# Pooled attention in slots of one unit, inputs laid out features first, one reduction per pooling sum

## The chip, the core and the metric

One core of a Trainium2 chip. The metric is device time in microseconds, the median of the runs shown; less is better. Engines are named as the profile names them: PE is TensorE (PEld its weight loads), DVE VectorE, ACT ScalarE, POOL GpSimd, SP SyncE, which here issues every DMA.

## The reference

Attention over pooled keys and values, then two gated layers. All inputs and the output are float32; shapes and factors as used:

```python
B, H, S, D = 8, 8, 576, 64          # pool = 8, so 72 pooled positions
k_p = k.reshape(B, H, 72, 8, D).mean(axis=3)
v_p = v.reshape(B, H, 72, 8, D).mean(axis=3)
attn = softmax(q @ k_p^T / sqrt(D)); x = attn @ v_p      # -> x: 4608 x 512
h = x @ w_in;  x = (h * sigmoid(1.702 h)) @ w_out         # 512 -> 2048 -> 512
out = ((x @ w_a) * (x @ w_b)) @ w_o2                      # 512 -> 1536 -> 512
```

## The kernel before

The 4608 tokens are 9 blocks j of 512, and a block is 4 units u of 128 tokens. The hidden features are split over four passes (`passes`): pass 0 makes features 0 to 5 (in 128s) of the first layer for all 9 blocks, pass 1 features 6 to 15, passes 2 and 3 the second layer. One step of pass 0 is one block and one 128-feature f: 12 matmuls of 512 columns into `h` (`emit_h`, L112 to L114: each product is made of hi and lo parts, three matmuls), the gate on ACT and DVE (L374, L375, split into `ghi` and `glo` by L71 and L72), and 12 matmuls into the accumulators `acc` (`emit_y`, the same three lines).

Attention runs inside pass 0, one block ahead of the steps that use it; units 0 to 3 run before the first step. A unit has five stages. `stage_a`: PE transposes q (tile `qt`, L211), ACT copies it to `qT` (L213). `stage_b1`: scores `sc` on PE against block-diagonal pooled keys `kbd` (L227), maximum on DVE (L234, L235), eight exponentials with row sums on ACT (L238). `stage_b2`: DVE normalises the weights `at` (L247 to L249). `stage_c`: PE transposes them (tile `pt`, L258), ACT copies to `aT` (L259). `stage_d`: PE multiplies with the pooled values (tile `px`, L271), and ACT and DVE split the result into the block's `xhi` and `xlo` (L71, L72). A unit that spans two batches does its scores and values in two pieces.

Keys and values are pooled per batch. `kv_ops` loads the raw rows of two heads at a time into `kraw` (two buffers for keys and values together, L188), and `sum_positions` adds the eight positions by halving: 512, 256 and 128 elements (L172, L172, L174). `stage_k` transposes the summed keys on PE (tile `kt`, L203) and copies them into `kbd` (L204, L205).

The stages of all units stand in one list, `unit_ops`: per unit the groups b1; b2 and the next unit's a; c; d. `spread` deals the list of a block evenly over the six steps of the block before. Weights come as 64-bit words and are converted by `convert`: eight DVE operations and one on ACT per half of a 128-feature tile (L93 to L109). Six such tiles are needed by the end of block 0. Every engine works its queue in order; the order in a queue is fixed when the program is built. SP issues all loads and stores in one queue, too.

Of the kernel before, what the change touches and what calls it, by code (L numbers as in the profile page):

```python
# [24 lines left out]
def tile_kernel(ctx, tc, q, k, v, w_in, w_out, w_a, w_b, w_o2, out):  # L25
# [129 lines left out]
    def last_batch(u):
        return min(B - 1, ((u + 1) * P - 1) // S)

    def load_q(u):
        t = ap_.tile([P, H, D], F32, tag="q", name="q", bufs=2)
        for o, n, b, s in pieces(u):  # L160
            nc.sync.dma_start(out=t[o:o + n], in_=q[b, :, s:s + n, :].rearrange("h p d -> p h d"))
        q_t[u] = t

    def kv_tiles(b):
        ks_t[b] = ap_.tile([SP, H, D], F32, tag="ks", name="ks", bufs=1)
        vs_t[b] = ap_.tile([SP, H, D], F32, tag="vs", name="vs", bufs=2)

    def sum_positions(dst, raw):

        n = POOL // 2  # L170
        while n > 1:
            nc.vector.tensor_tensor(out=raw[:, :, 0:n, :], in0=raw[:, :, 0:n, :], in1=raw[:, :, n:2 * n, :], op=ALU.add)  # L172
            n //= 2
        nc.vector.tensor_tensor(out=dst, in0=raw[:, :, 0, :], in1=raw[:, :, 1, :], op=ALU.add)  # L174

    def positions(src, b, h, n):
        return src[b, h:h + n].rearrange("h (p r) d -> p h r d", r=POOL)

    def kv_ops(b):

        waiting = []

        def one(src, tiles, h):
            if src is k and h == 0:
                kv_tiles(b)
            if src is not None:
                raw = ap_.tile([SP, 2, POOL, D], F32, tag="kraw", name="kraw", bufs=2)
                nc.sync.dma_start(out=raw, in_=positions(src, b, h, 2))  # L188
                waiting.append((tiles, h, raw))
            if len(waiting) > 1 or src is None:  # L190
                tiles, h, raw = waiting.pop(0)
                sum_positions(tiles[b][:, h:h + 2, :], raw)

        todo = [(src, tiles, h) for src, tiles in ((k, ks_t), (v, vs_t)) for h in range(0, H, 2)]
        return [lambda a=a: one(*a) for a in todo + [(None, None, None)]]

    def stage_k(b):


        ks = ks_t.pop(b)  # L200
        pt = ps.tile([P, NP, SP], F32, tag="ps", name="kt")
        for c in range(NP):
            nc.tensor.transpose(pt[:, c, :], ks[:, 2 * c:2 * c + 2, :].rearrange("p h d -> p (h d)"), ident[:SP, :SP])  # L203
        nc.scalar.copy(out=kbd[b % 2][0:D, :, 0:SP], in_=pt[0:D])  # L204
        nc.scalar.copy(out=kbd[b % 2][D:P, :, SP:2 * SP], in_=pt[D:P])  # L205

    def stage_a(u):
        t = q_t.pop(u)
        pt = ps.tile([P, NP, P], F32, tag="ps", name="qt")
        for c in range(NP):  # L210
            nc.tensor.transpose(pt[:, c, :], t[:, 2 * c:2 * c + 2, :].rearrange("p h d -> p (h d)"), ident)  # L211
        s = ap_.tile([P, NP, P], F32, tag="qT", name="qT", bufs=2)
        nc.scalar.copy(out=s, in_=pt)  # L213
        qT_t[u] = s

    def stage_b1(u):
        qT = qT_t.pop(u)
        a = ap_.tile([P, H, SP], F32, tag="at", name="at", bufs=2)
        mx = ap_.tile([P, H], F32, tag="mx", name="mx", bufs=2)
        sm = ap_.tile([P, H], F32, tag="sm", name="sm", bufs=2)  # L220
        scale = 1.0 / (POOL * D ** 0.5)
        for half in range(2):
            sc = ps.tile([P, H // 2, SP], F32, tag="ps", name="sc")
            for c in range(2):
                pair = 2 * half + c
                for o, n, b, s in pieces(u):
                    nc.tensor.matmul(  # L227
                        out=sc[o:o + n, 2 * c:2 * c + 2, :].rearrange("p h k -> p (h k)"),
                        lhsT=qT[:, pair, o:o + n],
                        rhs=kbd[b % 2][:, pair, :],  # L230
                        start=True, stop=True,
                    )
            hs = slice(half * (H // 2), (half + 1) * (H // 2))
            nc.vector.tensor_reduce(out=mx[:, hs], in_=sc, op=ALU.max, axis=AX.X)  # L234
            nc.vector.tensor_scalar_mul(mx[:, hs], mx[:, hs], -scale)  # L235
            for c in range(H // 2):
                h = half * (H // 2) + c
                nc.scalar.activation(  # L238
                    out=a[:, h, :], in_=sc[:, c, :], func=AF.Exp, scale=scale, bias=mx[:, h:h + 1],
                    accum_out=sm[:, h:h + 1],  # L240
                )
# [20 lines left out]
    def stage_d(u):  # L262
# [5 lines left out]
        for c in range(NP):  # L268
            for e in range(2):
                for o, w, b, s in pieces(u):  # L270
# [12 lines left out]
    stages = {"a": stage_a, "b1": stage_b1, "b2": stage_b2, "c": stage_c, "d": stage_d}  # L283
    loaded_q, made_b = [0], [0]

    def loads_to(u):
        while loaded_q[0] <= min(u, NU - 1):
            load_q(loaded_q[0])
            loaded_q[0] += 1

    def keys_for(u):
        while made_b[0] <= last_batch(u):
            stage_k(made_b[0])
            made_b[0] += 1
# [3 lines left out]
    unit_ops = []  # L298
    for u in range(NU):
        unit_ops += [[("b1", u)], [("b2", u)] + ([("a", u + 1)] if u + 1 < NU else []), [("c", u)], [("d", u)]]  # L300
    for b in range(2, B):
        i = 4 * (b * S // P) - 14
        for n, op in enumerate(kv_ops(b)):
            unit_ops[i + n * 3 // 2].insert(0, op)

    def ops_of(j):

        return [op for i in range(4 * UB * j, 4 * UB * (j + 1)) for op in unit_ops[i]]

    def step(op):  # L310
        if callable(op):
            op()
            return
        kind, u = op
        stages[kind](u)
        if kind == "a":
            keys_for(u)
            loads_to(u + 2)
# [170 lines left out]
    for j in range(1, NB):  # L489
        spread(([("a", UB)] if j == 1 else []) + ops_of(j), place[0, j - 1, 0], place[0, j, 0] - 1)  # L490
# [49 lines left out]
    def load_raw(src, b, n):  # L540
        raws = []
        for h in range(0, H, n):
            raw = wp.tile([SP, n, POOL, D], F32, tag="w", name="kvraw")
            nc.sync.dma_start(out=raw, in_=positions(src, b, h, n))
            raws.append((h, n, raw))
        return raws

    tmps += [ap_.tile([P, 512], U32, tag="tmp", name="tmp", bufs=3) for _ in range(3)]
    kv_tiles(0)
    kraws = load_raw(k, 0, 2)  # L550
    loads_to(1)
# [3 lines left out]
    for h, n, raw in kraws:
        sum_positions(ks_t[0][:, h:h + n, :], raw)
    step(("a", 0))
    step(("a", 1))
    for h, n, raw in vraws:
        sum_positions(vs_t[0][:, h:h + n, :], raw)  # L560
    stage_b1(0)
    stage_b1(1)
    stage_b2(0)
    stage_c(0)
    step(("a", 2))
    stage_d(0)
    stage_b2(1)
    stage_c(1)
    stage_d(1)
    make_w((1, 0), 0)  # L570
    make_w((1, 0), 1)
    stage_b1(2)
    load_w((1, 2))
    step(("a", 3))
    stage_b2(2)
    stage_b1(3)
    stage_c(2)
    stage_d(2)
    stage_b2(3)
    stage_c(3)  # L580
# [63 lines left out]
```

## Time and profile before

| | |
|---|---|
| median of 3 runs | 1944.31 us (1940.04 to 1946.99) |
| the profiled execution | 1944.94 us, of which the span is 1943.1 us |
| PE busy | 1845.0 us (95%) |
| DVE busy | 871.9 us (45%) |
| ACT busy | 561.5 us (29%) |
| DMA | 206.97 MB in 111552 packets, 43608 of them under 512 B |

The span is cut into 40 slices of 48.6 us in the profile; a digit there is a busy share in tenths, and PEclk is the granted TensorE clock in tenths of 2.4 GHz. Idle time of PE matters only where PE then has less to do than time; so the text reads the clock, the idle time and what ended it by stretch. A PE record is longer than its pace, since matmuls overlap: the pace is the distance between starts, and the chain of waits shows it as the length of a piece. The trace has two records for a matmul on plain float32 (scores, values), one for the others.

### The profile page before, as it was taken

Reading aid. Unit: us, or ns where it says so; the run is one execution under the profiler, and the core shown is the slowest. Engines: PE = TensorE matmul, PEld = TensorE weight load, DVE = VectorE, ACT = ScalarE, POOL = GpSimd, SP = SyncE. Lnnn points to the kernel's source line nnn. Section 1 sums busy time; section 2 is a strip of 40 time slices with the busy share of each in tenths; the row PEclk is TensorE's granted clock in tenths of the full one; section 3 lists DMA queues with packets and bytes.
Section 4 is the critical chain, followed back from the end, with each engine's and each line's share of the span. In section 5 each row is a group of like instructions: output and inputs, shape, how many; then the busy total and the mean of one; then the engine's idle time right before and its main releaser. Section 6 shows DMA issues by size and latency. Waiting matters only on the chain.

```text
span 1943.1 us, 22159 instructions
## 1 busy us (share of the span) xinstructions
PE 1845.0 (95%) x8768; PEld 1509.1 (78%) x8768; DVE 871.9 (45%) x1654; ACT 561.5 (29%) x1381; POOL 1.7 (0%) x8
## 2 busy tenths in 40 slices
PE   3698899889999999999999999999999999999998
PEld 2576777667788888888888888888888888888887
DVE  8955666555556444444544354444622212221221
ACT  4354454445533222232222122222211111111111
POOL 0000000000000000000000000000000000000000
PEclk8799999899999999999999999999999999999999
DMA  8533343432271222333322353424022102210200
GB/s 222 172 122 85 123 144 129 140 108 84 94 272 65 99 97 98 119 130 119 130 98 98 120 184 106 165 97 163 22 87 87 60 27 87 87 54 33 87 22 22
DMA packets 111552, 206.97 MB, mean 107 GB/s; under 512 B 43608, under 2 KB 64088, under 8 KB 99928
## 3 DMA queue, kind: packets, MB, share of 16 engines
q1 hardware_dynamic: 111448, 205.55, 30.9%
q8 instruction: 69, 1.13, 0.3%
q14 instruction: 35, 0.29, 0.0%
HBM read 139.46 MB, written 66.06 MB: 106 GB/s over the span
## 4 chain that ended last, share of the span: by engine, by line
PE 86%; DVE 6%; DMA 5%; ACT 2%; SPq 1%; issue 0%; DVEq 0%; ACTq 0%
PE ab L112 10%; PE ab L113 10%; PE ab L114 10%; PE h L112 6%; PE acc L112 6%; PE acc L113 6%; PE h L113 6%; PE h L114 6%; PE acc L114 6%; PE acc L413 5%; PE acc L414 5%; PE acc L415 5%; DMA kraw<-in_k_dram 2%; DMA kraw<-in_v_dram 2%; PE px L271 1%; DVE kraw L172 1%
## 5 line engine op out<-in xcount | busy, mean ns | idle before, releaser
L112 PE MATMUL ab<-xhi,w 128*128 128x512 f32 x864 | 336.1, 389 | 0.0
L113 PE MATMUL ab<-xlo,w 128*128 128x512 f32 x864 | 336.1, 389 | 0.0
L114 PE MATMUL ab<-xhi,w 128*128 128x512 f32 x864 | 336.1, 389 | 0.0
L401 DVE TENSOR_TENSOR c<-c,ab 128x512 f32<-128x512 f32 x108 | 74.3, 688 | 529.6 <-PE ab L114 529.6
L112 PE MATMUL h<-xhi,w 128*128 128x512 f32 x576 | 229.1, 401 | 6.8 <-ACT xhi L71 6.6
L113 PE MATMUL acc<-glo,w 128*128 128x512 f32 x576 | 229.6, 399 | 2.3 <-DVE glo L72 2.1
L113 PE MATMUL h<-xlo,w 128*128 128x512 f32 x576 | 228.0, 396 | 2.7 <-DVE xlo L72 2.7
L114 PE MATMUL acc<-ghi,w 128*128 128x512 f32 x576 | 227.2, 394 | 0.0
L114 PE MATMUL h<-xhi,w 128*128 128x512 f32 x576 | 226.9, 394 | 0.0
L375 DVE SCALAR_TENSOR_TENSOR g<-g,h 128x512 f32<-128x512 f32 x144 | 98.6, 685 | 250.7 <-ACT g L374 250.1
L112 PE MATMUL acc<-ghi,w 128*128 128x512 f32 x576 | 179.7, 405 | 12.5 <-ACT ghi L71 11.8
L114 PEld LDWEIGHTS ab<-xhi,w 128*128 128x128 f32 x864 | 162.2, 188 | 33.7
L112 PEld LDWEIGHTS ab<-xhi,w 128*128 128x128 f32 x864 | 162.2, 188 | 33.7
L113 PEld LDWEIGHTS ab<-xlo,w 128*128 128x128 f32 x864 | 162.2, 188 | 33.5
L374 ACT ACTIVATE g<-h 128x512 f32<-128x512 f32 x144 | 86.3, 600 | 303.8 <-PE h L114 291.3
L413 PE MATMUL acc<-w,chi 128*128 128x512 f32 x432 | 168.0, 389 | 0.0
L414 PE MATMUL acc<-w,chi 128*128 128x512 f32 x432 | 168.0, 389 | 0.0
L415 PE MATMUL acc<-w,clo 128*128 128x512 f32 x432 | 167.6, 389 | 0.0
L400 ACT COPY c<-ab 128x512 f32<-128x512 f32 x108 | 63.6, 589 | 356.4 <-PE ab L114 356.4
L71 ACT CAST chi<-c 128x512 fp32r<-128x512 f32 x108 | 66.9, 620 | 288.8 <-DVE c L401 288.8
L112 PEld LDWEIGHTS acc<-ghi,w 128*128 128x128 f32 x576 | 107.7, 193 | 37.2 <-ACT ghi L71 16.8
L112 PEld LDWEIGHTS h<-xhi,w 128*128 128x128 f32 x576 | 109.3, 191 | 32.2 <-ACT xhi L71 8.6
(66 smaller groups left out, 2162.9 us busy)
## 6 DMA issues: line engine op xcount, KB each, us to landing
part<-ys SPq DMA_DIRECT2D x72, 256.0 KB
part<-part SPq DMA_DIRECT2D x18, 1024.0 KB
xhi<-yd SPq DMA_DIRECT2D x18, 1024.0 KB
xlo<-yd SPq DMA_DIRECT2D x18, 1024.0 KB
xd<-xhi SPq DMA_DIRECT2D x9, 1024.0 KB
xd<-xlo SPq DMA_DIRECT2D x9, 1024.0 KB
xhi<-xd SPq DMA_DIRECT2D x9, 1024.0 KB
xlo<-xd SPq DMA_DIRECT2D x9, 1024.0 KB
```

The costliest lines, as they stand in the source:

```text
L71: nc.scalar.copy(out=hi, in_=src)
L112: nc.tensor.matmul(out=o, lhsT=whi, rhs=xhi, start=first, stop=False)
L113: nc.tensor.matmul(out=o, lhsT=whi, rhs=xlo, start=False, stop=False)
L114: nc.tensor.matmul(out=o, lhsT=wlo, rhs=xhi, start=False, stop=last)
L172: nc.vector.tensor_tensor(out=raw[:, :, 0:n, :], in0=raw[:, :, 0:n, :], in1=raw[:, :, n:2 * n, :], op=ALU.add)
L374: nc.scalar.activation(out=g, in_=hps, func=AF.Tanh, scale=0.5 * 1.702)
L375: made = nc.vector.scalar_tensor_tensor(out=g, in0=g, scalar=1.0, in1=hps, op0=ALU.add, op1=ALU.mult)
L400: nc.scalar.copy(out=cc, in_=pab[0])
L401: made = nc.vector.tensor_tensor(out=cc, in0=cc, in1=pab[1], op=ALU.mult)
L413: nc.tensor.matmul(out=o, lhsT=chi[:, cs], rhs=whi, start=first, stop=False)
L414: nc.tensor.matmul(out=o, lhsT=chi[:, cs], rhs=wlo, start=False, stop=False)
L415: nc.tensor.matmul(out=o, lhsT=clo[:, cs], rhs=whi, start=False, stop=last)
```

## The change

Before the launch the arrays are laid out anew on the host (`_laid_out`): q and k with features on the partitions, v with the eight positions innermost, and w_in, w_a, w_b so that a 128-feature tile is 4 KB in a row per partition. The bytes stay the same. In the kernel:

- `stage_a`, `stage_k`'s transposes and `qT` are gone: q is loaded as the scores need it, and `kbd` is filled from the sums.
- A pooling sum is one `tensor_reduce` of DVE over the innermost eight: for keys two per batch of 1152 elements on 128 partitions, for values four of 1024 on 72 (two of 2048 in batches 0 and 1).
- Raw keys and raw values have buffers of their own: one for keys, two for values. Converting has two scratch tiles instead of three.
- Attention goes in slots: slot t does scores of unit t, transposes of t-1, values of t-2. Loads of keys and values stand one slot or more ahead of their sum.

```diff
@@ the stages
+    def load_q(u, t=None):
+        q_t[u] = ap_.tile([P, NP, P], F32, tag="q", name="q", bufs=2) if t is None else t
+        nc.sync.dma_start(out=q_t[u], in_=q[u])
+
+    def load_k(b, half, raw=None):
+        if raw is None:
+            raw = ap_.tile([P, 2, S], F32, tag="kraw", name="kraw", bufs=1)
+        nc.sync.dma_start(out=raw, in_=k[b, :, 2 * half:2 * half + 2, :])
+        kraw_t[b, half] = raw
+
+    def sum_k(b, half):
+        ks = ap_.tile([P, 2, SP], F32, tag="ks", name="ks", bufs=1)
+        raw = kraw_t.pop((b, half)).rearrange("p c (s r) -> p c s r", r=POOL)
+        nc.vector.tensor_reduce(out=ks, in_=raw, op=ALU.add, axis=AX.X)
+        cs = slice(2 * half, 2 * half + 2)
+        nc.scalar.copy(out=kbd[b % 2][0:D, cs, 0:SP], in_=ks[0:D])
+        nc.scalar.copy(out=kbd[b % 2][D:P, cs, SP:2 * SP], in_=ks[D:P])
+
+    def load_v(b, h, n, raw=None):
+        if raw is None:
+            raw = ap_.tile([SP, n, D, POOL], F32, tag="vraw", name="vraw", bufs=2)
...
+        nc.vector.tensor_reduce(out=vs_t[b][:, h:h + n, :], in_=vraw_t.pop((b, h)), op=ALU.add, axis=AX.X)
@@ the order of attention
-    for u in range(NU):
-        unit_ops += [[("b1", u)], [("b2", u)] + ([("a", u + 1)] if u + 1 < NU else []), [("c", u)], [("d", u)]]
+    def slot(t, lo, hi):
+        todo = [
+            (t, op(stage_b1, t, 0)), (t - 1, op(stage_b2, t - 1)), (t - 2, op(stage_d, t - 2)),
+            (t, op(stage_b1, t, 1)), (t - 1, op(stage_c, t - 1)),
+        ]
+        return [o for u, o in todo if lo <= u < hi]
...
+        for t, ops in (
+            (u0 - 5, [op(load_k, b, 0)]), (u0 - 4, [op(sum_k, b, 0), op(load_k, b, 1), op(load_v, b, 0, V)]),
+            (u0 - 3, [op(sum_k, b, 1), op(load_v, b, V, V)]),
+            (u0 - 2, [op(sum_v, b, 0, V), op(load_v, b, 2 * V, V)]),
+            (u0 - 1, [op(sum_v, b, V, V), op(load_v, b, 3 * V, V)]),
+            (u0, [op(sum_v, b, 2 * V, V)]), (u0 + 1, [op(sum_v, b, 3 * V, V)]),
@@ the first four units (slots of their own, conversions between them)
+    for t, ops in enumerate(slots):
...
+        if t == 0:
+            make_w((1, 0), 0)
+        if t == 2:
+            make_w((1, 0), 1)
+            load_w((1, 3))
+        if t == 3:
+            make_w((1, 1), 0)
```

Three places in the order of the instructions. First PE in block 1 of pass 0, before: the transposes of a unit (`pt`), its values (`px`), and the scores (`sc`) of the next. `h` and `acc` are the matmuls of the steps.

```order
L258 MATMUL pt<-ident,at 72x128 x8
L112 MATMUL acc<-ghi,w 128x512 x4
L271 MATMUL px<-aT,vs 64x128 x4
L227 MATMUL sc<-kbd_123,qT 128x144 x4
L113 MATMUL acc<-glo,w 128x512
L114 MATMUL acc<-ghi,w 128x512
L113 MATMUL acc<-glo,w 128x512
L114 MATMUL acc<-ghi,w 128x512
L271 MATMUL px<-aT,vs 64x128 x4
L112 MATMUL h<-xhi,w 128x512
```

And after, about the same place:

```order
L200 MATMUL sc<-kbd_122,q 128x144 x2
L246 MATMUL px<-aT,vs 64x128 x8
L200 MATMUL sc<-kbd_122,q 128x144 x2
L233 MATMUL pt<-ident,at 72x128 x4
L111 MATMUL acc<-ghi,w 128x512 x2
L233 MATMUL pt<-ident,at 72x128 x4
L111 MATMUL acc<-ghi,w 128x512
L111 MATMUL h<-xhi,w 128x512
L112 MATMUL h<-xlo,w 128x512
```

The `px` are those of unit t-2 and the `pt` those of t-1, whose scores stood one slot earlier; before, the next `pt` in the queue are of the unit whose `sc` is shown here.

Second DVE, at a pooling sum beside a gate (`g`, `glo`); before:

```order
L172 TENSOR_TENSOR kraw<-kraw 72x2x256 x2
L172 TENSOR_TENSOR kraw<-kraw 72x2x128 x2
L174 TENSOR_TENSOR vs<-kraw 72x128
L247 TENSOR_SCALAR sm<-sm 128x8
L174 TENSOR_TENSOR vs<-kraw 72x128
L248 RECIPROCAL sm<-sm 128x8
L249 TENSOR_TENSOR at<-at,sm 128x576
L172 TENSOR_TENSOR kraw<-kraw 72x2x256
L172 TENSOR_TENSOR kraw<-kraw 72x2x128
L375 SCALAR_TENSOR_TENSOR g<-g,h 128x512
L172 TENSOR_TENSOR kraw<-kraw 72x2x256
L174 TENSOR_TENSOR vs<-kraw 72x128
```

After:

```order
L224 RECIPROCAL sm<-sm 128x8
L225 TENSOR_TENSOR at<-at,sm 128x576
L207 TENSOR_REDUCE mx<-sc 128x4
L337 SCALAR_TENSOR_TENSOR g<-g,h 128x512
L208 TENSOR_SCALAR mx<-mx 128x4
L170 TENSOR_REDUCE ks<-kraw 128x144
L71 TENSOR_TENSOR xlo<-px,xhi 128x4x128
L71 TENSOR_TENSOR glo<-g,ghi 128x512
L207 TENSOR_REDUCE mx<-sc 128x4
L337 SCALAR_TENSOR_TENSOR g<-g,h 128x512
```

Where a sum was three rows and a new load stood between pairs of them, there is one row on a tile of its own.

Third SP in block 0; before:

```order
L188 DMA kraw<-in_k_dram 72x2x512
L161 DMA q<-in_q_dram 128x8x64
L188 DMA kraw<-in_k_dram 72x2x512
L344 DMA raw<-in_moe_w_in_dram 128x4x256
L344 DMA raw<-in_moe_w_out_dram 128x1024
L344 DMA raw<-in_moe_w_in_dram 128x4x256
L344 DMA raw<-in_moe_w_out_dram 128x1024
L188 DMA kraw<-in_v_dram 72x2x512 x3
```

After:

```order
L162 DMA kraw<-in_k_dram 128x1152
L306 DMA raw<-in_moe_w_in_dram 128x1024
L306 DMA raw<-in_moe_w_out_dram 128x1024
L255 DMA xd_83<-xhi 128x2048
L256 DMA xd_83<-xlo 128x2048
L162 DMA kraw<-in_k_dram 128x1152
L306 DMA raw<-in_moe_w_in_dram 128x1024
L306 DMA raw<-in_moe_w_out_dram 128x1024
L156 DMA q<-in_q_dram 128x512 x2
L162 DMA kraw<-in_k_dram 128x1152
L156 DMA q<-in_q_dram 128x512
```

A load of keys (`kraw`, one buffer) stands ahead of weights (`raw`) and of q in the queue.

## Rows read from the trace of the kernel before

**Rows 1.** The granted clock by slice, from the page.
```profile
PEclk8799999899999999999999999999999999999999
```

**Rows 2.** By stretch: us, busy PE, PEld, DVE, ACT, POOL, then clock, DMA share, GB/s.
```profile
0.00:63.90 63.90, 21.89 (x148) 17.79 (x148) 53.49 (x120) 25.19 (x90) 1.74 (x8) 0.76 0.76 207
63.90:133.90 70.00, 59.81 (x320) 44.90 (x320) 48.26 (x112) 30.53 (x101) 0.00 (x0) 0.88 0.39 119
133.90:534.00 400.10, 359.46 (x2108) 284.00 (x2108) 234.70 (x534) 198.88 (x681) 0.00 (x0) 0.96 0.37 119
```

**Rows 3.** Chain of waits around 404 to 424 us: start, length, what.
```profile
402.96 0.59 PE px L271 x8
403.55 0.43 PE h L112
403.98 0.23 PE h L113
...
408.31 0.44 PE qt L211 x4
408.75 0.27 PE kt L203 x4
...
409.36 4.02 DMA kraw<-in_k_dram
...
416.78 4.19 DMA kraw<-in_v_dram
...
421.76 0.60 DVE g L375
...
422.39 0.63 ACT ghi L71
...
423.06 1.22 PE acc L112 x2
```

**Rows 4.** Who waited for whom on PE, blocks 1 to 7: us, times, longest.
```profile
PE pt L258 <- DVE at L249: 22.2, 11, 6.2
PE acc L112 <- ACT ghi L71: 9.1, 4, 4.7
PE h L112 <- ACT xhi L71: 5.2, 7, 1.1
PE px L271 <- ACT aT L259: 1.4, 5, 0.3
```

**Rows 5.** One stall on PE, in order of time; start, length, last the idle time before.
```profile
163.83 1.90 PE L258 MATMUL pt<-ident,at 128*72 128x128 f32 x8 [6.15 <-DVE at L249]
```

**Rows 6.** The same columns right behind two stalls of PE.
```profile
164.00:170.00 6.00, 6.00 (x20) 4.65 (x19) 2.22 (x4) 1.16 (x2) 0.00 (x0) 0.57 0.16 52
423.00:430.00 7.00, 6.94 (x30) 5.36 (x32) 4.51 (x10) 1.76 (x4) 0.00 (x0) 0.60 0.24 80
```

**Rows 7.** PE's transposes in blocks 1 to 7, by form.
```profile
L211 PE MATMUL qt<-ident,q 128*128 128x128 f32 x108 | 16.2, 273 | 0.0
L203 PE MATMUL kt<-ident,ks 72*128 72x72 f32 x24 | 2.5, 226 | 0.0
```

**Rows 8.** DVE's sums of raw rows and its maximum, by form, whole span.
```profile
L172 DVE TENSOR_TENSOR kraw<-kraw 72x512 f32<-72x512 f32 x48 | 32.9, 685 | 47.9 <-DMA kraw<-in_v_dram 25.7 <-DMA kraw<-in_k_dram 22.0
L172 DVE TENSOR_TENSOR kvraw<-kvraw 72x1024 f32<-72x1024 f32 x6 | 7.3, 1219 | 2.2 <-DMA kvraw<-in_v_dram 2.0 <-DMA kvraw<-in_k_dram 0.2
L234 DVE TENSOR_REDUCE mx<-sc 128x4 f32<-128x288 f32 x72 | 32.1, 451 | 11.9 <-PE sc L227 11.7
```

**Rows 9.** First step on PE, in order of time.
```profile
67.75 0.80 PE L113 MATMUL h<-xlo,w 128*128 128x512 f32 x1 [2.67 <-DVE xlo L72]
```

**Rows 10.** The gate of block 0's last step on DVE, in order of time.
```profile
127.00 0.69 DVE L375 SCALAR_TENSOR_TENSOR g<-g,h 128x512 f32<-128x512 f32 x1
```

**Rows 11.** First step of block 1 on PE, in order of time.
```profile
133.91 0.73 PE L112 MATMUL h<-xhi,w 128*128 128x512 f32 x2 [0.69 <-ACT xhi L71]
```

More of the change, by code (lines that the diff above doesn't have):

```diff
@@ L151, in pieces @@
             n = min(P - done, S - s)
-            yield done, n, b, s
+            yield done, n, b
             done += n
[L155 to L220, printed above, removed]
-        scale = 1.0 / (POOL * D ** 0.5)
[L222 to L240, printed above, removed]
-                )
-        at_t[u] = a, sm
@@ L269, in stage_d @@
             for e in range(2):
[L270 removed]
+                for o, w, b in pieces(u):
                     nc.tensor.matmul(
@@ L281, in stage_d, with op @@
             nc.sync.dma_start(out=xd[j][:, 1], in_=f32(lo))
[L283 to L298, printed above, removed]
-    for u in range(NU):
-        unit_ops += [[("b1", u)], [("b2", u)] + ([("a", u + 1)] if u + 1 < NU else []), [("c", u)], [("d", u)]]
-    for b in range(2, B):
[L302 to L318, printed above, removed]
+    def op(f, *a):
+        return lambda: f(*a)
+    def slot(t, lo, hi):
[4 more added lines that the diff above has]
+        return [o for u, o in todo if lo <= u < hi]
+    slots = [slot(t, 0, UB) for t in range(UB + 2)]
+    later = {t: slot(t, UB, NU) for t in range(UB, NU + 2)}
+    V = 2
+    for b in range(2, B):
+        u0 = b * S // P
+        for t, ops in (
[4 more added lines that the diff above has]
+            (u0, [op(sum_v, b, 2 * V, V)]), (u0 + 1, [op(sum_v, b, 3 * V, V)]),
+        ):
+            later[t] += ops
     w_t = {}
@@ L489, in tile_kernel @@
     for j in range(1, NB):
-        spread(([("a", UB)] if j == 1 else []) + ops_of(j), place[0, j - 1, 0], place[0, j, 0] - 1)
+        ts = range(UB if j == 1 else UB * j + 2, UB * (j + 1) + 2)
+        spread([o for t in ts for o in later[t]], max(0, place[0, j - 1, 0] - 1), place[0, j, 0] - 1)
     for i in range(1, 4):
@@ L537, in tile_kernel, with load_kv @@
     in_rooms(keys2[9:], place[3, 0, FA2], place[3, 0, NF2 - 2] - 1)
[L540 to L551, printed above, removed]
+    def load_kv(b):
+        for half in range(2):
+            load_k(b, half, wp.tile([P, 2, S], F32, tag="w", name="kvraw"))
+            yield
+        for h in range(0, H, H // 2):
+            load_v(b, h, H // 2, wp.tile([SP, H // 2, D, POOL], F32, tag="w", name="kvraw"))
+            yield
@@ L552, in tile_kernel @@
+    tmps += [ap_.tile([P, 512], U32, tag="tmp", name="tmp", bufs=2) for _ in range(2)]
+    qs = wp.tile([P, UB, NP, P], F32, tag="w", name="qs")
+    kv0, kv1 = load_kv(0), load_kv(1)
+    next(kv0)
+    load_q(0, qs[:, 0])
+    next(kv0)
     load_w((1, 0))
-    vraws = load_raw(v, 0, 4)
+    next(kv0)
+    load_q(1, qs[:, 1])
+    next(kv0)
+    load_q(2, qs[:, 2])
     load_w((1, 1))
[L555 to L572, printed above, removed]
-    load_w((1, 2))
[L574 to L580, printed above, removed]
-    stage_d(3)
-    make_w((1, 1), 0)
-    make_w((1, 1), 1)
-    load_w((1, 3))
@@ L599, in tile_kernel @@
-    for n, ops in enumerate(first_ops):
+    load_q(3, qs[:, 3])
+    next(kv1)
+    next(kv1)
+    load_w((1, 2))
+    next(kv1)
+    next(kv1)
+    for half in range(2):
+        sum_k(0, half)
+    for t, ops in enumerate(slots):
+        if t == 2:
+            for half in range(2):
+                sum_v(0, half * H // 2, H // 2)
+        for o in ops:
+            o()
+        if t == 0:
+            make_w((1, 0), 0)
+        if t == 2:
+            make_w((1, 0), 1)
+            load_w((1, 3))
+        if t == 3:
+            make_w((1, 1), 0)
```

97 lines of the change are left out of this document (66 added, 31 removed).

## Prediction

> **What bounds the kernel now.** I read the page's slices first: the granted clock is under 0.9 only in slices 1, 2 and 8 of 40 [rows 1], all in pass 0, where attention runs. What can be won lies there. The passes behind it are matmuls at PE's own pace, and nothing in the change touches them: weights and x are the same, only read in longer rows.
>
> Then the table by stretch [rows 2]. Up to the first step (0 to 63.9 us) DVE is busy 53.5 of 63.9 us and PE 21.9: DVE bounds it, with conversions, raw sums and softmax. In block 0 (63.9 to 133.9) PE works 59.8 of 70 us at clock 0.88, DVE 48.3. In blocks 1 to 7 (133.9 to 534.0) PE works 359.5 of 400.1 us at clock 0.96, DVE only 234.7. So there it is latency, not the throughput of any engine, that leaves 40.6 us idle, and 0.04 of 400.1 = 16.0 us go to the low clock.
>
> The list of waits says for what [rows 4]: 22.2 us for the normalised weights before the transposes `pt`, 9.1 us for `ghi`, 5.2 us for `xhi` at the first step of a block, 1.4 us for `aT`. One wait for `pt` is 6.15 us long [rows 5], and the 6 us after it run at 0.57; the same after the wait that ends at 423 us, 0.60 [rows 6]. That second stall is in the chain of waits [rows 3]: keys land after 4.02 us, values after 4.19 us, DVE stands at the head of its queue for them, and the gate `g`, then `ghi`, then `acc` come late behind. Over the span DVE waits 47.9 us for raw rows before its first additions [rows 8].
>
> **The change, part by part: blocks 1 to 7.**
>
> - q's transposes: 0.44 us for four [rows 3], 108 of them [rows 7]: 27 x 0.44 = 11.9 us of PE. Keys' transposes: 0.27 us for four, 24: 1.6 us. Together 13.5 us off the path, since PE has no other cover there. The copies after them leave ACT, which is busy 198.9 of 400.1 us [rows 2]: nothing.
> - The wait for `pt`. I counted, in PE's order, the PE work between the last score matmul of a unit and its first transpose, at the pace in the chain of waits (0.23 us for a matmul of 512 columns, 0.59 for eight of `px` [rows 3]): the median of units 8 to 35 is 5.9 us before (lowest 2.7) and 13.3 us after (lowest 8.1). Between them lie a maximum, eight exponentials and the normalisation in other engines' queues, for which 5.9 us is just too little. All 22.2 us go.
> - The wait for `ghi`: the same count between the end of an `h` and the first `acc` of that step gives a median of 3.8 us before and 6.8 us after over blocks 1 to 7. The shown 4.7 us hangs on raw rows whose load was issued two sums before; they now have a slot. I take 8 of 9.1 us, between the one shown and all.
> - The clock: it falls behind long stalls [rows 5, 6]. With nearly all of those gone I take 15 of 16.0 us.
> - The waits for `xhi` and `aT` stay: the last unit's `px` still stands just ahead of the next block's first `h`.
> - New waits: a pair of value sums is 3.4 to 4.6 us of DVE work ahead of the next pair, while a load lands 4.0 to 4.2 us after the sum that frees its buffer [rows 3]. At most about 1 us on DVE a pair, less than the 6.8 us of cover; if that cover were gone, some 5 us. I take 1 us.
>
> 13.5 + 22.2 + 8 + 15 - 1 = 57.7, so 400.1 becomes 342.4 us.
>
> **Start and block 0.** The price of the new sum is not in the trace as such. DVE's additions cost 685 ns for 512 and 1219 ns for 1024 elements, so 1.043 ns an element and 151 ns besides; on that line 288 elements give 451 ns, which is just what the maximum, the same `tensor_reduce` over 72 elements, takes [rows 8]. So 1152 elements of keys cost 1.35 us, 1024 of values 1.22 us, 2048 2.29 us. A batch falls from 8 x 1.39 = 11.1 us to 2 x 1.35 + 4 x 1.22 = 7.6 us, batches 0 and 1 together from about 19.4 to 14.6 us. The bounds: not below 1.35 us for 1152, as no float32 row of DVE is quicker per element with two inputs or a reduction; above, twice the line, if eight elements a group should cost restarts. The Trainium skill (page "VectorE: DVE Perf Modes", section "Rules for kernel authors") calls `tensor_reduce` the slowest DVE operation, to be restructured when it is on the hot path. By that rule taken as twice the price of an addition, the sum would be 22 us higher (second rival). The maximum on the line of the additions does not bear it out [rows 8].
>
> DVE's order up to the last `xlo` of unit 3, which the first step waits for [rows 9], holds 67.2 us of durations before (its end in the trace: 67.7 us) and 54.4 us now: 4.8 us less of sums, and five halves of weights converted ahead instead of seven. A DVE row lets the next begin before its end (the gate is 0.69 us long and holds the chain of waits for 0.60 [rows 3, 10]); by that the two lists take 57.2 and 47.5 us. The waits, 67.7 - 57.2 = 10.5 us, are mostly for the first loads, and I keep them: the first step at about 58 us, 10 us earlier. Loading is no new bound: what is needed for the first scores is half of k, then q and the other half, 1.4 MB, and 207 GB/s were moved in this stretch [rows 2], 7 us for 1.4 MB; before, the same keys came first, too.
>
> The two conversions not done ahead fall into block 0, and two slots more of attention with them: from there to the sixth gate DVE's list grows from 49.9 to 59.1 us of durations. At the same overlap (0.85) that is 50 us without waits, and 6.9 us more to block 1's first step, as before [rows 10, 11]: 58 + 50 + 6.9 = 114.9 us at the least. Before, it came at 133.9 us, with some 17 us of DVE waiting in block 0, mostly for raw rows and for PE. A queue that is full waits little: I take 1 us, so 115.9 us, 18 us earlier. Bounds: 111 us (the loads land 4 us sooner) to 124 us (half of the old waits).
>
> Two scratch tiles instead of three, one buffer for keys, the longer rows of the weights: nothing, since DVE works its conversions one after the other, the key sums lie mostly 4 to 25 us of DVE work apart, and DMA is busy 0.37 of blocks 1 to 7 [rows 2]. In block 0 DVE bounds, so a scratch tile that is late costs there; it is in the 124 us.
>
> **The sum.** The profiled execution took 1944.9 us, of which 1943.1 is the span; the median of the runs is 0.6 us below it. 1944.9 - 57.7 - 18 = 1869.2: **1869 us**. Block 8 and passes 1 to 3 stay as they are. With everything at its better bound (waits for `xhi` and `aT` gone as well) it is 1944.9 - 69 - 23 = 1853 us.
>
> **Rivals.**
>
> - *Half of the stalls come back* in another place: DVE goes to about 0.64 busy in blocks 1 to 7 and works in order, so a gate can still stand behind a conversion of eight rows. For: the lowest cover of a gate stays 2.7 us. Against: the medians. Half of 22.2 + 8 + 15: 1869 + 23 = 1892 us. Chance 0.20.
> - *The reduction costs twice the line.* Then DVE, the bound up to block 1, has 14.6 + 7.6 us more in batches 0 to 2; later it has the idle time. 1869 + 22 = 1891 us. This is the rule of the Trainium skill above; the maximum's row speak against it. Chance 0.08.
> - *Slower: loads exposed one by one.* SP works in order, and a load of keys waits there for the sum that frees the only key buffer, ahead of weights and q. If DVE comes to each sum before its load has landed, it stands 4.1 us [rows 3] for each of 6 x 6 loads, 148 us, with gates behind it; PE then waits as at 423 us. That is up to 2017 us, and it is slower than before once over 76 of the 148 us reach PE. It decides where DVE's work between a sum and the next on that buffer is under 4.1 us; in the order that is so for some of the value pairs, by less than 1 us, and hardly for keys. Chance 0.04.
> - *The slots do not separate the stages in time*, because the fixed order lets the exponentials pile up in ACT's queue: then only transposes and start remain, 1945 - 13.5 - 18 = 1913 us. The order of PE speaks against it. Chance 0.05.
> - *Everything at the better bound*: about 1853 us. Chance 0.13.
>
> My forecast has 0.50. A measurement of this kernel tells 0.3% (about 6 us) from no change. Faster by more: all but the slower rival, 0.95; within it 0.01; slower 0.04. The range runs from just under the better bound, 1848 us, to above the first two rivals with a late block 0, 1906 us; about 0.15 is left outside.
>
> **What would show it.** Right: no `pt` among PE's waits worth over 3 us in blocks 1 to 7; the clock at 0.99 or 1.00 there; the first step of block 1 near 116 us; a key sum of 1.35 us; blocks 1 to 7 in 342 us, passes 1 to 3 unchanged. Wrong: waits of DVE for raw rows that stay near 48 us (third rival), a key sum near 2.6 us (second), or PE waits for `ghi` over 20 us (first).

## The result and the profile after

The kernel after takes **1853.01 us** (median of 4 runs, 1851.01 to 1855.16), the kernel before beside it 1945.42 us (4 runs): a ratio of **0.953, 95% interval 0.9507 to 0.9552**. The forecast was 1869 us in a range of 1848 to 1906. So the direction and the range held, and the time came out 16 us below the likeliest value, at the 1853 us of the rival with everything at its better bound; but not in that rival's way, as the stretches show.

The profiled execution took 1854.09 us. From its page, the granted clock by slice:

```profile
PEclk8789999999999999999999999999999999999999
```

Slice 8 is no longer under 0.9 [rows 1]; slices 1 to 3 are, the third newly so. By stretch, with the columns of [rows 2]: start, block 0, blocks 1 to 7, and the rest:

```profile
0.00:58.20 58.20, 24.30 (x128) 18.69 (x128) 45.36 (x86) 24.36 (x91) 1.73 (x8) 0.79 0.75 229
58.20:126.60 68.40, 59.05 (x320) 45.60 (x321) 55.96 (x119) 35.90 (x138) 0.00 (x0) 0.83 0.49 161
126.60:443.50 316.90, 316.33 (x1955) 259.52 (x1954) 211.80 (x432) 177.11 (x624) 0.00 (x0) 1.00 0.41 141
443.50:1852.30 1408.80, 1403.66 (x6193) 1161.95 (x6191) 534.30 (x889) 306.42 (x509) 0.00 (x0) 1.00 0.27 98
```

Beside [rows 2]: the start is 5.7 us shorter, block 0 only 1.6 us, blocks 1 to 7 83.2 us, and the rest 0.3 us (1409.1 before). Together 90.8 us, the difference of the two spans. In blocks 1 to 7 PE idles 0.6 of 316.9 us where it idled 40.6, at clock 1.00 where it had 0.96: this stretch now goes at PE's pace. In the list of who waited for whom on PE, one row is left there, where [rows 4] had four:

```profile
PE pt L233 <- ACT at L211: 0.5, 1, 0.5
```

The sums, by form over the whole span (busy us, mean ns, then the idle time before them):

```profile
L184 DVE TENSOR_REDUCE vs<-vraw 72x128 f32<-72x1024 f32 x24 | 28.4, 1210 | 9.9 <-DMA vraw<-in_v_dram 9.8
L170 DVE TENSOR_REDUCE ks<-kraw 128x144 f32<-128x1152 f32 x12 | 16.2, 1348 | 5.3 <-DMA kraw<-in_k_dram 5.2
L184 DVE TENSOR_REDUCE vs<-kvraw 72x256 f32<-72x2048 f32 x4 | 9.1, 2280 | 3.3 <-DMA kvraw<-in_v_dram 3.2
```

1210, 1348 and 2280 ns stand where the line through the additions [rows 8] gave 1.22, 1.35 and 2.29 us. The idle time for `kraw` and `vraw` is 15.0 us, against 47.9.

Block 0 is another matter. On PE, in order of time, its first step and the stalls (idle time before in brackets):

```profile
58.28 1.22 PE L111 MATMUL h<-xhi,w 128*128 128x512 f32 x2 [0.69 <-ACT xhi L70]
...
73.27 0.79 PE L112 MATMUL acc<-glo,w 128*128 128x512 f32 x1 [3.32 <-DVE glo L71]
...
100.52 2.07 PE L111 MATMUL acc<-ghi,w 128*128 128x512 f32 x4 [3.16 <-ACT ghi L70]
...
104.28 0.80 PE L112 MATMUL acc<-glo,w 128*128 128x512 f32 x1 [1.69 <-DVE glo L71]
```

The first step begins at 58.3 us; the forecast of 58 us was made for the end of the last `xlo` (taken up below). The first step of block 1 stands at 126.67 us, 7 us earlier than before [rows 11] and not 18. The chain of waits names what is behind the stalls at 100 and 104 us:

```profile
90.31 11.06 DMA vraw<-in_v_dram
101.39 1.22 DVE vs L184
...
103.67 0.57 DVE glo L71
104.28 0.80 PE acc L112
105.08 0.43 PE acc L113
```

A load of values of 288 KB takes 11.06 us here, where [rows 3] has 4.02 and 4.19. The columns of [rows 2] for the time in which it is under way, and behind it:

```profile
90.30:101.40 11.10, 7.94 (x49) 6.33 (x47) 8.65 (x19) 5.32 (x21) 0.00 (x0) 0.90 0.87 265
101.40:108.00 6.60, 4.91 (x12) 3.20 (x12) 4.70 (x10) 1.32 (x8) 0.00 (x0) 0.50 0.19 53
```

The DMA engines are busy 0.87 of that time: SP had issued q, two tiles of weights in four loads and another load of values in the 2.7 us before it. With the load itself that is 2.95 MB, and 2.95 MB at the 265 GB/s of this stretch are 11.1 us (an estimate, as if all of it moved in this stretch). And behind the stalls the granted clock is 0.50, the lower level (1.2 GHz).

### The profile page after: what moved, and what is told of

The parts are those of the page before. It is cut to its first block, busy times and chain, and to the rows that moved or that the text cites. A ratio compares the mean times of both kernels' runs of the same rounds, so it can differ in the third digit from the quotient of the medians.

```text
span 1852.3 us, 21637 instructions
## 1 busy us (share of the span) xinstructions
PE 1803.3 (97%) x8592; PEld 1485.8 (80%) x8592; DVE 847.4 (46%) x1524; ACT 543.8 (29%) x1361; POOL 1.7 (0%) x8
## 4 chain that ended last, share of the span: by engine, by line
PE 94%; DMA 3%; DVE 2%; ACT 0%; issue 0%; SPq 0%; DVEq 0%; ACTq 0%
PE ab L112 11%; PE ab L111 11%; PE ab L113 11%; PE acc L112 7%; PE acc L111 7%; PE acc L113 7%; PE h L111 7%; PE h L112 7%; PE h L113 7%; PE acc L376 5%; PE acc L375 5%; PE acc L377 5%; PE sc L200 2%; PE px L246 2%; PE pt L233 2%; DMA kraw<-in_k_dram 1%
## 5 line engine op out<-in xcount | busy, mean ns | idle before, releaser
L113 PE MATMUL acc<-ghi,w 128*128 128x512 f32 x576 | 227.6, 395 | 0.0
L111 PE MATMUL h<-xhi,w 128*128 128x512 f32 x576 | 226.2, 394 | 0.7 <-ACT xhi L70 0.7
L113 PE MATMUL h<-xhi,w 128*128 128x512 f32 x576 | 224.6, 390 | 0.0
L111 PE MATMUL acc<-ghi,w 128*128 128x512 f32 x576 | 187.6, 401 | 3.9 <-ACT ghi L70 3.8
L112 PEld LDWEIGHTS acc<-glo,w 128*128 128x128 f32 x576 | 109.3, 190 | 28.4 <-DVE glo L71 6.2
```

The costliest lines, as they stand in the source:

```text
L111: nc.tensor.matmul(out=o, lhsT=whi, rhs=xhi, start=first, stop=False)
L112: nc.tensor.matmul(out=o, lhsT=whi, rhs=xlo, start=False, stop=False)
L113: nc.tensor.matmul(out=o, lhsT=wlo, rhs=xhi, start=False, stop=last)
```

## The experiments

Two explanations of the 83 us in blocks 1 to 7 were put against each other. A: it is the slots, by the PE work that they put between a producer and its consumer (the cover). B: it is what goes with them, raw rows with places and buffers of their own, cheaper sums, fewer transposes. The other runs price single parts and ask what block 0 is bound by. Ratios are to the kernel before on the same chip (median there 1945.79 us for the first four below, 1946.88 for the two that move more to GpSimd, 1943.62 for the others). An edit can change the order in the queues in more than the edited place.

**After without slots** (stages of a unit one behind the other from unit 4 on; loads and sums of values one slot earlier, the last sum two, since the values are used earlier; all else as after):

```diff
-    later = {t: slot(t, UB, NU) for t in range(UB, NU + 2)}
+    def unit(t):
+        todo = [op(stage_b1, t, 0), op(stage_b1, t, 1), op(stage_b2, t), op(stage_c, t), op(stage_d, t)]
+        return todo if t < NU else []
+
+    later = {t: unit(t) for t in range(UB, NU + 2)}
...
-            (u0 - 2, [op(sum_v, b, 0, V), op(load_v, b, 2 * V, V)]),
-            (u0 - 1, [op(sum_v, b, V, V), op(load_v, b, 3 * V, V)]),
-            (u0, [op(sum_v, b, 2 * V, V)]), (u0 + 1, [op(sum_v, b, 3 * V, V)]),
...
+            (u0 - 2, [op(sum_v, b, V, V), op(load_v, b, 3 * V, V)]),
+            (u0 - 1, [op(sum_v, b, 2 * V, V), op(sum_v, b, 3 * V, V)]),
...
```

> The changed kernel with its stages in the old order from unit 4 on: scores, normalisation, transposes and values of a unit one behind the other, no slots. Layouts, reductions and loads as in the change (value loads two slots earlier, since the values are used earlier). By PE's order the work between a unit's last score and its first transpose has a median of 4.9 us (13.3 with slots), that between an h and its acc 3.5 us (6.8). Theory A, the slots make the cover: waits for pt of 15 to 25 us and for ghi of 5 to 10 us come back in blocks 1 to 7, with low clock behind them; 1885 to 1915 us. Theory B, what helped is that DVE no longer stands for raw rows: the waits stay small, 1850 to 1863 us.

Measured: 1941.72 us, ratio 0.9986 (0.9972 to 0.9999). Nearly everything is given back, more than was expected. Its blocks 1 to 7, by stretch and by who waited for whom on PE:

```profile
127.70:527.80 400.10, 349.14 (x1977) 270.27 (x1977) 220.82 (x448) 185.72 (x661) 0.00 (x0) 0.96 0.35 116
```

```profile
PE pt L233 <- DVE at L225: 23.1, 12, 4.3
PE acc L111 <- ACT ghi L70: 16.5, 11, 3.9
PE h L111 <- ACT xhi L70: 5.5, 8, 0.7
PE acc L112 <- DVE glo L71: 4.2, 5, 2.3
PE px L246 <- ACT aT L234: 1.9, 7, 0.3
```

The stretch is as long as before to a tenth of a us, though PE has no transposes of q and k to do. PE is busy 10 us less [rows 2] and waits 51.2 instead of 37.9 us [rows 4]: what was taken off PE had been cover. The same count as in the prediction gives a median of 4.9 us of PE work ahead of `pt` and 3.5 us ahead of `acc`, where after has 13.3 and 6.8.

**Before with slots alone** (old layouts, transposes and sums):

```diff
-    for u in range(NU):
-        unit_ops += [[("b1", u)], [("b2", u)] + ([("a", u + 1)] if u + 1 < NU else []), [("c", u)], [("d", u)]]
+    def late(kind, u):
+        return [(kind, u)] if UB <= u < NU else []
+
+    for t in range(NU + 2):
+        unit_ops += [late("b1", t), late("b2", t - 1) + late("a", t + 1) * (t >= UB), late("d", t - 2), late("c", t - 1)]
...
```

> The kernel before with the slots alone, from unit 4 on: scores of t, values of t-2, transposes of t-1; layouts, transposes of q and k, halving additions and loads of raw rows as before. PE's order gives a median cover of 17.1 us before pt and 5.4 us before acc. Theory A: the 22 us of waits for pt go, and most of the low clock, 1900 to 1915 us; DVE's waits for raw rows stay near 40 us in blocks 1 to 7 but cost PE little. Theory B, raw rows at the head of DVE's queue are what stops PE: over 1925 us, with waits for ghi above 9 us.

Measured: 1889.67 us, ratio 0.9717 (0.9694 to 0.974), better than expected. Its blocks 1 to 7, and the raw rows' part of DVE's waits in them:

```profile
134.20:479.00 344.80, 335.87 (x2075) 274.30 (x2074) 223.98 (x510) 188.82 (x644) 0.00 (x0) 0.99 0.42 134
```

```profile
DVE kraw L172 <- DMA kraw<-in_k_dram: 15.3, 12, 2.8
DVE kraw L172 <- DMA kraw<-in_v_dram: 13.8, 11, 2.1
```

DVE still stands 29.1 us for raw rows in the shared buffers (39.5 before), and PE idles only 8.9 us; no wait of PE for `pt` on DVE or for `ghi` is left. So A holds for most of it: the stalls need the cover. B does not fall whole, though. Of the 8.9 us 8.0 are waits for the gate `g`, as `sc` and `h` take over the buffer that the gate reads; the three longest of them, 6.6 us together, each stand behind 2.3 to 2.5 us of DVE waiting for keys. The first of the three:

```profile
217.59 1.14 DVE L172 TENSOR_TENSOR kraw<-kraw 72x512 f32<-72x512 f32 x2 [2.47 <-DMA kraw<-in_k_dram]
...
220.11 0.63 DVE L379 SCALAR_TENSOR_TENSOR g<-g,h 128x512 f32<-128x512 f32 x1
...
220.80 1.21 PE L227 MATMUL sc<-kbd,qT 128*128 128x144 f32 x4 [2.50 <-DVE g L379]
```

So with cover, late raw rows cost PE some 6.6 us and not 29.1, besides the clock behind them (0.99). 56 of the 92 us are the slots by themselves.

**After with q transposed on PE again** (q loaded token by token, `stage_a` put into the slot ahead):

```diff
+    def stage_a(u):
+        t = q_t.pop(u)
+        pt = ps.tile([P, NP, P], F32, tag="ps", name="qt")
+        for c in range(NP):
+            nc.tensor.transpose(pt[:, c, :], t[:, c, :], ident)
+        s = ap_.tile([P, NP, P], F32, tag="qT", name="qT", bufs=2)
+        nc.scalar.copy(out=s, in_=pt)
...
-            (t, op(stage_b1, t, 0)), (t - 1, op(stage_b2, t - 1)), (t - 2, op(stage_d, t - 2)),
+            (t, op(stage_b1, t, 0)), (t - 1, op(stage_b2, t - 1)), (t + 1, op(stage_a, t + 1)),
+            (t - 2, op(stage_d, t - 2)),
...
```

> The changed kernel, but q is loaded tokens first and transposed on PE and copied by ACT as before, one slot ahead of its scores. If PE's pace bounds blocks 1 to 7 (its idle time there is 0.6 us), 36 units at 0.44 us come back in full: plus 13 to 17 us, 1866 to 1870 us. Rival 1, they hide in idle time: plus 0 to 4 us. Rival 2, the extra PSUM tile and the copies on ACT bring new waits: over 1878 us.

Measured: 1862.03 us, ratio 0.9575 (0.9554 to 0.9597), 9 us more than after. By stretch, block 0 and blocks 1 to 7:

```profile
62.50:120.70 58.20, 53.51 (x340) 42.89 (x341) 49.11 (x102) 36.81 (x134) 0.00 (x0) 0.97 0.50 165
120.70:451.20 330.50, 330.03 (x2061) 271.33 (x2061) 216.41 (x437) 192.48 (x659) 0.00 (x0) 1.00 0.40 137
```

Blocks 1 to 7 are 13.6 us longer. In them stand 100 records of the transposes, 25 units, and six more matmuls of block 0's end, 1.4 us at 0.23. So some 12.2 us, 0.49 a unit, are the price of the transposes: with the stalls gone, PE work counts in full. The start is 4.3 us longer, but block 1's first step comes 5.9 us earlier, with more PE work ahead of it. Up to there DVE is busy 99.9 us (101.3 in the kernel after), of which 5.4 more in the start and 6.9 less in block 0; so it waits less, and block 0's clock is 0.97 instead of 0.83. No theory had expected that, and the time lies between two of them.

**Before with long rows of weights alone** (w_in, w_a, w_b laid out as after):

```diff
-        return words[name][:, f * P:(f + 1) * P, :].rearrange("(k p) f w -> p k f w", p=P)
+        return words[name][f * P:(f + 1) * P, :, :]
...
+    if name in ("moe_w_in", "moe2_w_a", "moe2_w_b"):
+        r, c = a.shape
+        return a.reshape(r // 128, 128, c // 128, 128).transpose(2, 1, 0, 3).reshape(c, r)
...
```

> The kernel before with nothing changed but the layout of w_in, w_a and w_b, so that these loads have rows of 4 KB. My prediction: worth nothing, 1941 to 1949 us. Rival: the start waits for loads, and they land sooner, 1930 to 1938 us.

Measured: 1944.18 us, ratio 0.9992 (0.998 to 1.0004): nothing, as the prediction had it. This was tried in the kernel before alone.

**Every sum twice** (the same reduction two times into the same tile, for values as for keys):

```diff
-        nc.vector.tensor_reduce(out=ks, in_=raw, op=ALU.add, axis=AX.X)
+        for _ in range(2):
+            nc.vector.tensor_reduce(out=ks, in_=raw, op=ALU.add, axis=AX.X)
...
```

> The changed kernel with every pooling reduction done twice, one behind the other. It adds 7.6 us to DVE per batch, 14.6 us for batches 0 and 1. Theory: DVE's list bounds up to the first step of block 1 and nowhere later. Up to there stand the doubles of batches 0 to 2 and one or two of batch 3, some 23 us, at 0.85 some 15 to 22 us later; blocks 1 to 7 stay at 320 us with PE waits under 3 us: 1868 to 1875 us. Rival 1, DVE's queue is at its limit in blocks 1 to 7 as well: over 1885 us. Rival 2, DVE does not bound the start: under 1860 us.

Measured: 1871.87 us, ratio 0.9629 (0.9613 to 0.9645), 19 us more than after. By stretch:

```profile
0.00:68.00 68.00, 21.13 (x128) 15.88 (x128) 59.12 (x93) 24.05 (x91) 1.73 (x8) 0.92 0.64 196
68.00:135.50 67.50, 55.84 (x312) 42.85 (x313) 64.94 (x128) 35.48 (x136) 0.00 (x0) 0.88 0.46 158
135.50:460.50 325.00, 320.29 (x1961) 259.94 (x1961) 241.82 (x460) 177.97 (x626) 0.00 (x0) 1.00 0.41 139
```

9.8 us come in the start, none in block 0, and 8.1 us in blocks 1 to 7 (325.0 us, where 320 had been expected): PE idles 4.7 us there. The start is 9.8 us longer with 13.8 us more of DVE's work, so DVE bounds it in the main. Block 0 takes DVE's 9 us more without being longer, as its idle time shrinks from 12.4 to 2.6 us: its length in the kernel after is not that of DVE's list alone. And in blocks 1 to 7 the cover is enough for the sums as they are, not for twice their length.

**Work moved from DVE to GpSimd.** First the sums of batch 1, as additions by halving:

```diff
+    def halve(raw, dst):
+        for n in (4, 2):
+            nc.gpsimd.tensor_tensor(
+                out=raw[:, :, :, 0:n], in0=raw[:, :, :, 0:n], in1=raw[:, :, :, n:2 * n], op=ALU.add
+            )
+        nc.gpsimd.tensor_tensor(out=dst, in0=raw[:, :, :, 0], in1=raw[:, :, :, 1], op=ALU.add)
...
+        if b == 1:
+            halve(raw, ks)
...
```

> The changed kernel with the pooling sums of batch 1 on GpSimd, by halving additions, instead of DVE. It takes 7.3 us off DVE's list ahead of block 1. Theory: 4 to 6 us less, 1847 to 1849 us. Rival: GpSimd is late for unit 4's scores or slows DVE while it adds, no gain or a loss, 1853 to 1865 us.

Measured: **1843.56 us, ratio 0.9486 (0.9472 to 0.95)**, better than expected and the lowest of all, though two runs below cannot be told from it by the ratio. By stretch:

```profile
0.00:55.00 55.00, 24.00 (x129) 17.98 (x129) 48.26 (x85) 24.43 (x91) 21.55 (x20) 0.78 0.75 243
55.00:114.50 59.50, 54.34 (x312) 41.88 (x313) 53.16 (x113) 34.45 (x136) 0.00 (x0) 0.89 0.56 186
114.50:432.50 318.00, 318.00 (x1962) 260.49 (x1961) 213.04 (x435) 178.20 (x626) 0.00 (x0) 1.00 0.40 141
```

3.2 us of the gain are in the start and 8.9 in block 0; 1.1 us go back in blocks 1 to 7. In block 0 DVE's waits for values are gone, and with them the stalls that the kernel after has at 100 and 104 us; one of 3.3 us early in the block, for `ghi` instead of `glo`, is left. Block 1's first step stands at 114.5 us, where the prediction had 116.

The expected reason, a shorter list of DVE, is not what the trace shows: up to block 1's first step DVE is busy 101.4 us, and 101.3 in the kernel after. It is DVE's idle time that fell, from 25.3 to 13.1 us. One more thing differs: SP now issues the two loads of values ahead of the two tiles of weights, which stood ahead of them in the kernel after:

```profile
83.43 1.45 SPq L188 DMA_DIRECT2D vraw<-in_v_dram  x2
84.98 0.35 SPq L319 DMA_DIRECT2D raw<-in_moe_w_in_dram  x1
```

Then one DVE operation of each of the first twelve half tiles of weights as two GpSimd operations:

```diff
+            if side:
+                nc.gpsimd.tensor_scalar(out=f32(low), in0=low, scalar1=2.0 ** -52, scalar2=None, op0=ALU.mult)
+                nc.gpsimd.tensor_tensor(out=f32(low), in0=f32(low), in1=f32(high), op=ALU.mult)
...
```

> The changed kernel with one of the eight DVE operations of a conversion (the low word times its scale, 0.69 us) done as two operations of GpSimd in the first 12 halves. It takes 8.2 us off DVE's list ahead of block 1. Theory: 5 to 7 us less, 1846 to 1848 us. Rival: the two operations on GpSimd take longer than the DVE work they stand beside, and the last addition waits, 1853 to 1870 us.

Measured: 1849.52 us, ratio 0.9513 (0.9499 to 0.9527); 3.5 us less than after by the medians, but the intervals overlap, and less was gained than expected. GpSimd takes 2.04 and 1.68 us for the two operations, which DVE did in 0.68 as one.

Two attempts to get more out of the first. The sums of batches 1 and 2 on GpSimd (`if b in (1, 2)`):

> The changed kernel with the pooling sums of batches 1 and 2 on GpSimd by halving additions. Batch 1 alone gave 9.4 us. Batch 2 takes another 7.6 us off DVE ahead of block 1; GpSimd needs 20 us a batch and has time for it. Theory: 1837 to 1841 us. Rival: batch 2's sums gate the scores of units 9 and later, or block 0 is held by PE's stalls and low clock and no longer by DVE's list: 1843 to 1850 us.

Measured: 1847.61 us, ratio 0.9487 (0.9471 to 0.9502), no better than batch 1 alone, as the rival had it. And batch 1's sums together with the conversion's operation from the sixth to the twelfth half tile:

> The changed kernel with the pooling sums of batch 1 on GpSimd and, from the sixth half of a weight tile to the twelfth, one DVE operation of the conversion as two on GpSimd (3.7 us there for 0.69 us of DVE, seven times). Theory: a little less than batch 1 alone, 1839 to 1843 us. Rival: the conversions then wait for GpSimd behind the sums, 1844 to 1852 us.

Measured: 1849.52 us, ratio 0.9496 (0.9482 to 0.951): the second adds nothing to the first, again the rival.

**Loads and sums of keys one slot later:**

```diff
-            (u0 - 5, [op(load_k, b, 0)]), (u0 - 4, [op(sum_k, b, 0), op(load_k, b, 1), op(load_v, b, 0, V)]),
-            (u0 - 3, [op(sum_k, b, 1), op(load_v, b, V, V)]),
+            (u0 - 4, [op(load_k, b, 0)]), (u0 - 3, [op(sum_k, b, 0), op(load_k, b, 1), op(load_v, b, 0, V)]),
+            (u0 - 2, [op(sum_k, b, 1), op(load_v, b, V, V)]),
```

> The changed kernel with the loads and sums of keys, from batch 2 on, one slot later. It takes the key sums of batch 3 (2.7 us) out of block 0 and brings each closer to its use. Theory: 0 to 3 us less, 1850 to 1853 us. Rival: sums now come late for the scores, waits for the copies into kbd, over 1856 us.

Measured: 1851.86 us, ratio 0.9526 (0.9512 to 0.954): no difference from after that can be told.

## Why the prediction was right, and where it was not

**Right: the mechanism and most of its terms.** The transposes are worth some 12.2 us in blocks 1 to 7 by the run that puts q's back (forecast 11.9 for q). The 22.2 us for `pt` went, by the cover that was counted; without slots they are back as 23.1. The clock in blocks 1 to 7 is 1.00. The sums cost what the line said. Here the Trainium skill ("VectorE: DVE Perf Modes", section "Rules for kernel authors") had spoken against the change, as it calls `tensor_reduce` the slowest DVE operation; the run decides against that for float32: 1024 elements in 1210 ns, against 1219 ns for an addition of 1024 [rows 8]. The page gives no factor; the doubled price of the second rival was the prediction's own reading. Long rows are worth nothing, and the rest of the kernel stayed as it was.

**Wrong: 116 us for block 1's first step; it was 126.67, 10.8 us later than the sum's 115.9.** Two steps failed: a small one in the start, where the waits are "mostly for the first loads, and I keep them"; and the main one, "In block 0 DVE bounds" with what follows from it, "A queue that is full waits little: I take 1 us". The forecast of 58 us for the first step is by its working the end of the last `xlo`, 67.7 us before. The first matmul needs `xhi` alone, and came at 63.9 before and at 58.3 now; the last `xlo` is here:

```profile
59.46 0.68 DVE L71 TENSOR_TENSOR xlo<-px,xhi 128x512 fp32r<-128x512 f32 x1
```

It ends at 60.14 us, 2.1 late. Up to there, and from there to the sixth gate, which starts at 120.39 us, with the columns of [rows 2]:

```profile
0.00:60.14 60.14, 26.15 (x136) 19.90 (x138) 47.30 (x90) 24.39 (x91) 1.73 (x8) 0.79 0.75 230
60.14:120.39 60.25, 50.98 (x272) 39.36 (x269) 50.27 (x106) 31.81 (x124) 0.00 (x0) 0.82 0.48 158
```

In the start DVE is busy 47.3 us, as the sum had it (47.5), and waits 12.8 us where the prediction kept 10.5. Up to the gate it is busy 50.3 us, where the sum had 50, but waits 10.0 us where the sum had 1. From the gate to block 1's first step it is 6.3 us (6.9 in the sum). So DVE's list was sized rightly, and the waits were not: those of block 0 are 9.0 of the 10.8 us. Nor does the list alone bound block 0, as the run with every sum twice shows. In the whole block DVE stood 68.4 - 55.96 = 12.4 us: by its list of waits 4.3 for scores, 2.5 each for the gate and for values, 2.2 for the exponentials.

Two things were left out of those waits. A load was taken as 4.0 to 4.2 us, and one took 11.06 us behind two tiles of weights, at a DMA share of 0.87. And the price of PE's lower clock was left out of block 0: at 0.50 behind a stall of 3 us the scores come late, then DVE waits for them; in the chain of waits a matmul of 512 columns takes 0.43 us there instead of 0.23. How much of the 9 us is the one and how much the other stays open, as no run changes the order of SP's queue alone. The runs at hand speak for that order: in the kernel after, and with keys one slot later, weights are issued between or right ahead of the first two loads of values in block 0, and DVE waits 2.5 and 2.0 us for values. In the runs with sums twice, with q's transposes and with work on GpSimd these loads are issued first or 5 us and more behind the weights, and that wait is at most 1.0 us. In the last two kinds block 1's first step comes earlier, at 114.5 to 122.2 us (124.0 with keys later).

**Wrong: 342.4 us for blocks 1 to 7; it was 316.9, 25.5 less.** The step "The waits for `xhi` and `aT` stay: the last unit's `px` still stands just ahead of the next block's first `h`" failed: 6.6 us. In a slot the values (`px`) are followed by half of the scores and the transposes of the other unit; the chain of waits at the end of block 0 shows it:

```profile
121.03 1.02 PE px L246 x16
122.05 0.69 PE sc L200 x4
122.74 0.44 PE pt L233 x4
123.63 0.44 PE pt L233 x4
124.07 0.93 PE acc L111 x4
```

From the end of these `px` to the first `h` at 126.67 there are 4.6 us of PE work. Another 2.6 us are the rest of `ghi`, the clock and the new waits, where I had stayed short of the bounds; for `ghi` the reason was wrong too, as raw rows alone were not it: without slots DVE waits only 10.9 us for them, and PE 16.5 us for `ghi`. Of the 16.3 us that remain, 2.7 are idle time that [rows 2] has and [rows 4] does not list. Some 3.6 us are a term that the sum left out: attention runs two slots further ahead, so the scores of two units (16 of 248 records) and the `pt` of one (8 of 224) now lie in block 0, 4 x 0.69 + 2 x 0.44 us by the pieces above. The prediction put these slots on DVE's list in block 0 and did not take them off PE here. Part of the other 10 us shows in attention's own records in that stretch. Before:

```profile
L258 PE MATMUL pt<-ident,at 128*72 128x128 f32 x224 | 33.6, 300 | 23.0 <-DVE at L249 22.2 <-ACT qT L213 0.6
L271 PE MATMUL px<-aT,vs 72*64 72x128 f32 x400 | 32.3, 286 | 1.2 <-ACT aT L259 1.2
```

After:

```profile
L233 PE MATMUL pt<-ident,at 128*72 128x128 f32 x216 | 30.8, 272 | 0.5 <-ACT at L211 0.5
L246 PE MATMUL px<-aT,vs 72*64 72x128 f32 x400 | 27.2, 278 | 0.0
```

The 400 records of `px` keep PE 32.3 us before and 27.2 after; with slots alone it is 27.6 us, without slots 32.7. How the rest divides, and how much of this is the clock's term over again, stays open.

The two errors, +10.8 and -25.5 us, make nearly all of the 15 us by which the profiled execution (1854.09) is under the sum (1869.2). The sign was right for the reason that was given; that the time fell into the range is partly luck, as the errors have opposite signs.

**The rivals.** Slots that do not separate the stages, and stalls that come back elsewhere: both fell, as PE idles 0.6 us in blocks 1 to 7; block 0 keeps 9.4 us of idle time (10.2 before). The doubled price of a sum fell by its row; had it been so, the run with every sum twice says it would have cost 19 us (I had 22). Loads exposed one by one: DVE waits 10.8 us for raw rows in blocks 1 to 7 and PE pays nothing; but the one load of block 0 that took 11 us is this rival's mechanism, in a place where it had not been looked for. Rows of block 0 in the kernel before would not have told it: a load of keys that SP issued there at 102.90 us was no longer waited for at 106.26. What could have told it is the order of SP's queue after the change, by the megabytes just ahead of a load that DVE will wait for. The better bound has an error of its own: its 69 us are 67.4 by the terms listed (57.7, 6.6 for `xhi` and `aT`, and 3.1 that had been held back), so 1854.5 us and not 1853; no chance hangs on it.

## What to carry to other kernels

Where every engine works a fixed queue in order and no engine is full, count the work that stands in the bound engine's queue between a producer and its consumer, and put stages a slot apart until that exceeds the chain between them; here 13.3 instead of 5.9 us took away the waits for `pt`, and with the loads' own buffers all stalls of blocks 1 to 7 and the low clock behind them. Until that is done, work taken off the bound engine can be worth nothing, as it had been cover (without slots 0.9986, with them q's transposes are worth some 12 us). Price a load by what stands ahead of it in its queue, and a wait by rows of the stretch in which it will lie.

## What was not expected of the hardware

GpSimd beside DVE. In the run with batch 1's sums on GpSimd, its additions by form:

```profile
L167 POOL TENSOR_TENSOR kvraw<-kvraw 128x576 f32<-128x576 f32 x2 | 7.5, 3750 | 20.0 <-DMA kvraw<-in_k_dram 20.0
L167 POOL TENSOR_TENSOR kvraw<-kvraw 72x1024 f32<-72x1024 f32 x2 | 5.1, 2572 | 0.0
```

1024 elements take 2572 ns, 2.1 times DVE's 1219 [rows 8]; and 576 elements took longer than 1024, though both are read in the same steps (four of every eight). The form is not what made it so: with batch 2's sums on GpSimd too, an addition of 576 took half of that.

```profile
44.49 1.79 POOL L167 TENSOR_TENSOR kraw<-kraw 128x576 f32<-128x576 f32 x1
```

So how long a GpSimd row is depends on what stands beside it: while the first one ran (from 22.30 us), DVE's rows of 512 elements kept their 0.68 us. Later DVE's rows stretch (in order of time):

```profile
33.14 2.31 DVE L221 TENSOR_SCALAR mx<-mx 128x4 f32<-128x4 f32 x1
...
35.96 2.32 DVE L98 SCALAR_TENSOR_TENSOR tmp<-raw,tmp 128x512 uint32<-128x512 uint32 x1
...
39.65 0.44 DVE L220 TENSOR_REDUCE mx<-sc 128x4 f32<-128x288 f32 x1
```

An operation on 4 elements takes 2.31 us, where it takes 0.15 in the kernel after; one on 512 takes 2.32 instead of 0.68; the reduction keeps its 0.44 us. The Trainium skill ("SBUF — State Buffer", section "Who interferes with whom") says that the two engines share a pair of ports as an exclusive lock, which an operation holds to its end, and that `tensor_reduce` on trn2 never contends for it; these rows agree with both. Up to block 1's first step DVE is busy 101.4 us with batch 1's sums on GpSimd and 101.3 in the kernel after, though 7.3 us of sums (two keys, two values at the prices above) were taken off its list. That may be why more work on GpSimd brought nothing more; it was not tried apart.
